# Four-slice tiles for the MoE activations, and a fixed place for the query products, in a linear-attention + MoE kernel

## The chip, the cores and the metric

The kernel runs on one core of a Trainium2 chip. The metric is device time in microseconds (us) of one execution; the median of three runs is compared. A profiled execution is one more run with the hardware profiler on; its trace lists each instruction with its engine, start, duration and what it waited for. The engines are TensorE (PE, with its weight loads listed apart as PEld), VectorE (DVE), ScalarE (ACT), GpSimd (POOL) and SyncE (SP), whose queue issues the DMAs.

## The reference, cut to what matters

There are 8 batches with 8 heads of 576 positions and 64 dimensions; a feature has 128 columns, the model 512, the hidden layer 1024.

```python
def phi(x):
    proj = np.einsum('bhsd,df->bhsf', x, w_phi)
    proj = proj - np.max(np.abs(proj), axis=-1, keepdims=True)
    return np.concatenate([np.exp(proj), np.exp(-proj)], axis=-1)
q_p, k_p = (phi(q), phi(k))
kv = np.einsum('bhsf,bhsd->bhfd', k_p, v)
z = np.sum(k_p, axis=2)
num = np.einsum('bhsf,bhfd->bhsd', q_p, kv)
den = np.einsum('bhsf,bhf->bhs', q_p, z)[..., None] + 1e-06
x = num / den                       # heads side by side: (8, 576, 512)
...
h = np.maximum(x @ w_in, 0.0)
conv_out = sum over k of conv_w[k] * h shifted by k - 1 along the positions
gate = 1.0 / (1.0 + np.exp(-conv_out))
out = h * gate @ w_out
```

## The kernel before

**Attention.** A unit is two head pairs of a batch (16 units, `2 * b + qd`), cut into 5 groups of positions; a group has the running number j. For the keys, `k_process` projects a group (`kp`, lines 223 to 225), takes both exponentials (`ke`) and multiplies them with v into the sums `kv` in PSUM (lines 275 and 279). For the queries, `q_process` projects with two passes over a PSUM tile (lines 360 and 364), finds the largest magnitude of each position on DVE and ACT (lines 368 to 379), and a DMA writes these maxima back into two rows of the operand (line 380, `qx<-qmp`). A third pass on PE then subtracts them in PSUM (line 386). ACT takes the exponentials (line 397) and splits them into a high part and, with DVE, a low part (`qh`, `ql`, lines 60 and 65). The products of the queries with kv (`nm`, lines 418 and 426) follow, and the kv products of the keys five groups later are chained in between them with `after`. ACT copies denominator and numerators out (lines 444 and 449), a DMA spreads the denominator (`den<-dr`, line 447), and `x_process` divides and splits the result into `xh` and `xl`. The first four units project in another way, without a third pass, so third passes exist for the groups 20 to 79.

**MoE.** A part n is half of a batch's positions (288, with one more on either side for the convolution: 290). `h_part` computes eight slices of 128 hidden columns, 12 matmuls each (line 499), and ACT evacuates each from PSUM with a Relu into a tile `h` of its own (line 506); there are `NH` = 11 such tiles, and before slice `8 n + f` is evacuated the planner waits for the gate of slice `8 n + f - 11` (line 504). `conv_process` runs the convolution of each slice on POOL and DVE into `c`, one tile of eight slices (lines 522 and 527), one sigmoid over all eight on ACT (line 531), the product with h slice by slice on DVE (line 535), and the split into `gh` (ACT, line 60) and `gl` (DVE, line 65) slice by slice (line 544). `gh` and `gl` are tiles of four slices with two buffers each, so a part's halves take the places of the part before, once `o_part` has read these. `o_part` computes the output in four blocks of 24 matmuls (line 558), which ACT evacuates (`os`, line 563) and a DMA writes out. `moe_process` runs h_part(n) before o_part(n - 1).

**The order.** Each of these processes is a generator. A planner at the end of the function keeps a model clock `now` and steps one process at a time, by what is ready (`until`, `set_ready`) and by how much attention and MoE work is left; the instructions are recorded in that order, with priorities. The scheduler of the framework then lays out each engine's queue by these priorities and its own timeline model, and sets the semaphores; buffers are given out as it goes. An edge added by hand with `behind(ins, other)` only fixes the order of two instructions on one engine. Before the change there is one such edge per group: the third pass of group j comes behind the first pass of group j + 1 (lines 363 and 388).

Of the kernel before, what the change touches and what calls it, by code (L numbers as in the profile page):

```python
# [7 lines left out]
F32 = mybir.dt.float32  # L8
F32R = mybir.dt.float32r
I32 = mybir.dt.int32  # L10
U32 = mybir.dt.uint32
AF = mybir.ActivationFunctionType
ALU = mybir.AluOpType
# [7 lines left out]
TC = 288  # L21
HW = TC + 2
VW = D + 1
NH = 11

WINDOW = 16
LAT = 1.7
# [8 lines left out]
def kernel(  # L36
# [20 lines left out]
    def split(src, hi, lo, eng_hi, eng_lo):  # L57

        if eng_hi is nc.scalar:
            nc.scalar.activation(out=hi, in_=src, func=AF.Copy)  # L60
        elif eng_hi is nc.gpsimd:
            nc.gpsimd.tensor_scalar(out=hi, in0=src, scalar1=1.0, scalar2=0.0, op0=ALU.mult, op1=ALU.add)  # L62
        else:
            nc.vector.tensor_copy(out=hi, in_=src)
        eng_lo.tensor_tensor(out=lo, in0=src, in1=hi.bitcast(F32), op=ALU.subtract)  # L65
# [108 lines left out]
    def until(*keys):  # L174
        return ("until", [k for k in keys if k is not None])

    def set_ready(key, ns=0):
        ready[key] = now[0] + ns * LAT
# [140 lines left out]

    den = {}  # L320
    numt = {}
    firsts, third = {}, {}

    def behind(ins, other):

        tc.add_manual_dep(ins.ins, other.ins.name,
                          mybir.DependencyInfo(mybir.DependencyClass.NoSync, mybir.DependencyReason.DATA),
                          reason="a group's third pass behind the next group's first")
    xh, xl = {}, {}

    def q_process(b, qd, g):
# [11 lines left out]
        if lo is None:  # L343
            pr = project(n, hi, lo, b, qd, g, "q")
            yield pe(330 * n)
            yield wait(1700)
            yield until(back("num", 2))
            set_ready(("tp", *divmod(j, 5)))

            tp = pg.tile([P, 2, n, P], F32, name=f"tp{b}_{qd}_{g}", tag="gq", bufs=2)  # L350
            for t in range(n):
                for i in range(2):
                    nc.tensor.transpose(out=tp[:, i, t, :], in_=pr[:, 2 * t + i, :], identity=idn)
            yield pe(220 * n)
        else:
            x = hi
            tp = pg.tile([P, 2, n, P], F32, name=f"qp{b}_{qd}_{g}", tag="gq", bufs=2)
            tpf, xf = tp.rearrange("p i t s -> p (i t s)"), x.rearrange("p i s -> p (i s)")
            c = w // 32
            first = nc.tensor.matmul(out=tpf, lhsT=wq_hi, rhs=xf, start=True, stop=False, skip_group_check=True)  # L360
            firsts[j] = first
            if j - 1 in third:
                behind(third.pop(j - 1), first)
            nc.tensor.matmul(out=tpf, lhsT=wq_lo, rhs=xf, start=False, stop=False, skip_group_check=True)

            mt = sb.tile([P, 4, 16], F32, name=f"qmt{b}_{qd}_{g}", tag="qmt", bufs=2)
            with tc.high_priority():
                nc.vector.tensor_reduce(out=mt[:, 0, 0:c], in_=tpf.rearrange("p (c f) -> p c f", f=32), axis=AX,
                                        op=ALU.max, apply_absolute_value=True, apply_transpose=True)
                for a in range(1, 4):  # L370
                    nc.scalar.activation(out=mt[0:32, a, 0:c], in_=mt[32 * a : 32 * a + 32, 0, 0:c], func=AF.Copy)
                m = sb.tile([32, 32], F32, name=f"qm{b}_{qd}_{g}", tag="qm", bufs=2)
                mp = mx[j % 2]
                mr = mt[0:32, :, 0:c].rearrange("p a c -> p c a")
                nc.vector.tensor_reduce(out=mp[:, 0:c].bitcast(F32R), in_=mr, axis=AX, op=ALU.max)
                nc.vector.tensor_reduce(out=m[:, 0:c], in_=mr, axis=AX, op=ALU.max)
                nc.vector.tensor_tensor(out=mp[:, c : 2 * c].bitcast(F32R), in0=m[:, 0:c], in1=mp[:, 0:c], op=ALU.subtract)
                mpt = sb.tile([32, 32], F32, name=f"qmp{b}_{qd}_{g}", tag="qmp", bufs=2)
                nc.vector.transpose(out=mpt, in_=mp)
                nc.sync.dma_start(out=xf[D : D + 2, :].bitcast(F32).rearrange("k (c t) -> k c t", t=32), in_=mpt[0 : 2 * c, :])  # L380
            yield pe(230 * n)
            yield wait(4000)
            yield until(back("num", 2))
            set_ready(("tp", *divmod(j, 5)))
            with tc.high_priority():
                third[j] = nc.tensor.matmul(out=tpf, lhsT=wq_m, rhs=xf, start=False, stop=True, skip_group_check=True)
            if j + 1 in firsts:
                behind(third.pop(j), firsts[j + 1])
            yield pe(115 * n)
        f32 = 2 * b + qd < NKV_F32 or g == 0  # L390
        qh = sb.tile([P, 2, 2, n * P], F32 if f32 else F32R, name=f"qh{b}_{qd}_{g}", tag="qh", bufs=2)
# [18 lines left out]
        for pr_, o, s0, w in parts:  # L410
            for i in range(2):
                khi, klo, kf = kv[b, qd][i]
                k = 0
                for s in range(2):
                    c_ = slice(pr_ * VW, (pr_ + 1) * VW)
                    a, x = (kf if f32 else khi)[:, s, c_], qh[:, s, i, o : o + w]
                    if f32:
                        ins = after(ins, lambda: nc.tensor.matmul(out=ps[:, i, o : o + w], lhsT=a, rhs=x,
                                                                  start=(s == 0), stop=(s == 1)))
                        if paired:  # L420
                            for _ in range(n):
                                ins = after(ins, lambda: next(kvgen[j + 5], ins))
                        continue
                    l, y = klo[:, s, c_], ql[:, s, i, o : o + w]
                    for w_, x_ in ((a, x), (a, y), (l, x)):
                        ins = after(ins, lambda: nc.tensor.matmul(out=ps[:, i, o : o + w], lhsT=w_, rhs=x_,  # L426
                                                                  start=(k == 0), stop=(k == 5)))
                        k += 1
                        if paired and k % 3 > 0:
                            ins = after(ins, lambda: next(kvgen[j + 5], ins))  # L430
                yield pe(6 * max(w / 2.4, 55) + (4 * 160 if paired else 0))
# [56 lines left out]
    def h_part(n):  # L488
        b, c = divmod(n, 2)
        yield until(*[("x", b, p, c) for p in range(4)], "w_in")  # L490
        spawn(conv_process(n))
        for f in range(8):
            ps = pm.tile([P, HW], F32, name=f"hp{n}_{f}", tag="m")
            k = 0
            for p in range(4):
                xa, xb = xh[b, p, c], xl[b, p, c]
                wa, wb = win_hi[p][:, f * P : (f + 1) * P], win_lo[p][:, f * P : (f + 1) * P]
                for w_, x_ in ((wa, xa), (wa, xb), (wb, xa)):
                    nc.tensor.matmul(out=ps, lhsT=w_, rhs=x_, start=(k == 0), stop=(k == 11))  # L499
                    k += 1  # L500
                if p % 2 == 1:
                    yield pe(740)
            if 8 * n + f >= NH:
                yield until(("gate", 8 * n + f - NH))
            hs = sb.tile([P, HW], F32, name=f"h{n}_{f}", tag="h", bufs=NH)
            nc.scalar.activation(out=hs, in_=ps, func=AF.Relu)  # L506
            ht[n, f] = hs
            set_ready(("hs", n, f), 500)
        set_ready(("h", n))

    def conv_process(n):
        c = n % 2
        o = 0 if c == 0 else HW - TC
        for f in range(8):
            yield until(("hs", n, f), ("g4", n - 1) if n > 0 else None)
            if f == 0:
                c4 = sb.tile([P, 8, TC], F32, name=f"c{n}", tag="c", bufs=1)
            hs = ht.pop((n, f))
            ct[n, f] = hs, c4
            cv = c4[:, f, :]  # L520

            nc.gpsimd.tensor_scalar(out=cv, in0=hs[:, o : o + TC], scalar1=cw[:, f, 1:2], scalar2=0.0,  # L522
# [6 lines left out]
                                               op0=ALU.mult, op1=ALU.add)  # L529
        yield wait(2000)  # L530
        nc.scalar.activation(out=c4, in_=c4, func=AF.Sigmoid)  # L531
        for f in range(8):
            set_ready(("gate", 8 * n + f))
            hs, c4 = ct[n, f]
            nc.vector.tensor_tensor(out=c4[:, f, :], in0=c4[:, f, :], in1=hs[:, o : o + TC], op=ALU.mult)
        yield wait(3000)
        yield until(("o", n - 1) if n > 0 else "w_out")
        for f in range(8):
            hs, c4 = ct.pop((n, f))
            if f % 4 == 0:  # L540
                gh4 = sb.tile([P, 4, TC], F32R, name=f"gh{n}_{f}", tag="gh", bufs=2)
                gl4 = sb.tile([P, 4, TC], F32R, name=f"gl{n}_{f}", tag="gl", bufs=2)
            gt[n, f] = gh4[:, f % 4, :], gl4[:, f % 4, :]
            split(c4[:, f, :], *gt[n, f], nc.scalar, nc.vector)
        set_ready(("g4", n))
        set_ready(("g", n), 3000)

# [165 lines left out]
```

## Time and profile before

| | |
|---|---|
| median of 3 runs | 838.35 us (834.71 to 839.17) |
| profiled execution, its own time | 837.11 us |
| its span in the trace | 835.3 us |
| mean granted TensorE clock | 0.984 |
| busy: PE, DVE, ACT, POOL | 781.6, 666.5, 635.3, 310.3 us |

The span runs from the first to the last instruction; the time of the execution also has what lies around it, 1.8 us here. Busy time is the union of an engine's instructions, so overlaps count once, and a PE that is busy throughout can still differ in how closely its matmuls follow each other. A row of instructions names the line, the engine, the operation, the tiles (written <- read), the shape and the count.

### The profile page before, as it was taken

How to read it: one execution, taken by the hardware profiler on the slowest of the kernel's cores; microseconds unless marked ns; L12 is line 12 of the kernel's file. 1: busy time of each engine (PE TensorE's matmuls, PEld its weight loads, DVE VectorE, ACT ScalarE, POOL GpSimd, SP SyncE). 2: the span in 40 equal slices, each digit the busy share in tenths (PEclk: the TensorE clock that was granted, in tenths of full speed). 3: DMA queues.
4: the chain of work that ended last, by engine and by line, in shares of the span. 5: the costliest groups of instructions: out<-in, count | busy, mean ns of one | idle time of the engine just before them, and what ended most of it. 6: DMA issues, size and time to landing. Idle time of an engine off the chain costs nothing.

```text
span 835.3 us, 17596 instructions
## 1 busy us (share of the span) xinstructions
PE 781.6 (94%) x5972; PEld 746.7 (89%) x5972; DVE 666.5 (80%) x1570; ACT 635.3 (76%) x1468; POOL 310.3 (37%) x395
## 2 busy tenths in 40 slices
PE   7888889799999999988999899999999999999998
PEld 7776789799989898988999899899999999999998
DVE  6898998888868878888879688887987978766551
ACT  4787877959878897887888878888797888844332
POOL 5765463252524434233344242433424232211110
PEclk9998989999999999999999999999999999999999
DMA  5643422112221222222222221212221110000001
GB/s 167 183 131 113 126 75 77 48 38 65 62 64 53 63 80 76 67 69 60 77 66 74 71 68 54 73 56 69 62 81 54 56 46 23 11 30 29 22 22 43
DMA packets 66817, 56.46 MB, mean 68 GB/s; under 512 B 17832, under 2 KB 64680, under 8 KB 66728
## 3 DMA queue, kind: packets, MB, share of 16 engines
q1 hardware_dynamic: 66728, 55.35, 22.9%
q8 instruction: 47, 0.77, 0.4%
q14 instruction: 42, 0.34, 0.1%
HBM read 45.21 MB, written 9.44 MB: 65 GB/s over the span
## 4 chain that ended last, share of the span: by engine, by line
PE 32%; ACT 13%; DVE 9%; issue 4%; DMA 4%; POOL 1%; SPq 1%; ACTq 0%; POOLq 0%; DVEq 0%
PE op L558 12%; PE hp L499 11%; PE nm L426 3%; PE kv L279 3%; DVE c L527 2%; ACT qe L397 2%; DMA den<-dr 2%; ACT qh L60 1%; DVE ql L65 1%; ACT gh L60 1%; ACT dr L444 1%; ACT num L449 1%; ACT qx L199 1%; ACT c L531 1%; ACT L397 1%
## 5 line engine op out<-in xcount | busy, mean ns | idle before, releaser
L279 PEld LDWEIGHTS kv<-v,ke 128*128 128x128 f32 x1024 | 157.2, 195 | 10.6 <-ACT ke L260 3.4
L279 PE MATMUL kv<-v,ke 128*128 128x65 f32 x1024 | 163.6, 256 | 2.4 <-ACT ke L260 2.2
L527 DVE SCALAR_TENSOR_TENSOR c<-h,cw,c 128x288 f32<-128x288 f32 (+1 forms) x256 | 143.8, 572 | 26.2 <-POOL c L522 24.6
L499 PE MATMUL hp<-xh,win_hi 128*128 128x290 f32 x512 | 154.5, 303 | 4.6 <-ACT os L563 3.0
L558 PE MATMUL op<-gh,wout_hi 128*128 128x288 f32 x512 | 152.8, 299 | 2.4 <-ACT os L563 2.4
L499 PE MATMUL hp<-xl,win_hi 128*128 128x290 f32 x512 | 152.9, 299 | 0.0
L499 PE MATMUL hp<-xh,win_lo 128*128 128x290 f32 x512 | 152.5, 298 | 0.0
L558 PE MATMUL op<-gh,wout_lo 128*128 128x288 f32 x512 | 152.0, 297 | 0.0
L558 PE MATMUL op<-gl,wout_hi 128*128 128x288 f32 x512 | 151.9, 297 | 0.0
L522 POOL TENSOR_SCALAR c<-h,cw 128x288 f32<-128x288 f32 x128 | 81.5, 640 | 183.5 <-ACT h L506 145.0
L200 POOL TENSOR_TENSOR qx<-qr,qx 64x512 fp32r<-64x512 f32 (+1 forms) x60 | 75.5, 1258 | 162.8 <-ACT qx L199 144.5
L65 DVE TENSOR_TENSOR ql<-qe,qh 128x512 fp32r<-128x512 f32 x112 | 86.5, 788 | 27.0 <-ACT qh L60 26.8
L499 PEld LDWEIGHTS hp<-xh,win_hi 128*128 128x128 f32 x512 | 97.4, 191 | 7.6 <-ACT os L563 4.7
L558 PEld LDWEIGHTS op<-gh,wout_hi 128*128 128x128 f32 x512 | 96.7, 189 | 3.7 <-ACT os L563 3.1
L499 PEld LDWEIGHTS hp<-xl,win_hi 128*128 128x128 f32 x512 | 97.9, 191 | 0.4
L499 PEld LDWEIGHTS hp<-xh,win_lo 128*128 128x128 f32 x512 | 97.7, 191 | 0.4
L558 PEld LDWEIGHTS op<-gh,wout_lo 128*128 128x128 f32 x512 | 96.9, 189 | 0.4
L558 PEld LDWEIGHTS op<-gl,wout_hi 128*128 128x128 f32 x512 | 96.8, 189 | 0.4
L62 POOL TENSOR_SCALAR kxh<-kr 128x256 fp32r<-128x256 f32 (+1 forms) x80 | 40.5, 507 | 119.5 <-PE kp L224 50.5
L65 DVE TENSOR_TENSOR gl<-c,gh 128x288 fp32r<-128x288 f32 x128 | 55.5, 485 | 22.6 <-ACT gh L60 22.5
L506 ACT ACTIVATE h<-hp 128x290 f32<-128x290 f32 x128 | 50.4, 404 | 30.3 <-PE hp L499 29.8
L426 PE MATMUL nm<-ql,kvh 128*65 128x256 f32 x224 | 69.2, 309 | 2.2 <-DVE ql L65 2.2
(99 smaller groups left out, 1936.4 us busy)
## 6 DMA issues: line engine op xcount, KB each, us to landing
qr<-in_qT_dram SPq DMA_DIRECT2D x112, 128.0 KB
v<-in_vt_dram SPq DMA_DIRECT2D x80, 130.0 KB
out_dram<-os SPq DMA_DIRECT2D x64, 144.0 KB
kr<-in_kT_dram SPq DMA_DIRECT2D x64, 128.0 KB
w_r<-in_w_in_dram SPq DMA_DIRECT2D x8, 512.0 KB
w_r<-in_w_out_dram SPq DMA_DIRECT2D x8, 512.0 KB
rr<-rc SPq DMA_DIRECT2D x128, 2.2 KB
qr<-in_qT_dram SPq DMA_DIRECT2D x28, 64.0 KB
```

The costliest lines, as they stand in the source:

```text
L60: nc.scalar.activation(out=hi, in_=src, func=AF.Copy)
L62: nc.gpsimd.tensor_scalar(out=hi, in0=src, scalar1=1.0, scalar2=0.0, op0=ALU.mult, op1=ALU.add)
L65: eng_lo.tensor_tensor(out=lo, in0=src, in1=hi.bitcast(F32), op=ALU.subtract)
L200: nc.gpsimd.tensor_tensor(out=x[D:P], in0=raw[D:P], in1=x[D:P].bitcast(F32), op=ALU.subtract)
L279: ins = nc.tensor.matmul(out=kp[i][:, s, p0 : p0 + VW], lhsT=lhsT, rhs=v[:, (2 * t + i) * VW : (2 * t + i + 1) * VW], start=False, stop=(g ...
L397: nc.scalar.activation(out=e, in_=tps, func=AF.Exp, scale=1.0 - 2.0 * s)
L426: ins = after(ins, lambda: nc.tensor.matmul(out=ps[:, i, o : o + w], lhsT=w_, rhs=x_, start=(k == 0), stop=(k == 5)))
L499: nc.tensor.matmul(out=ps, lhsT=w_, rhs=x_, start=(k == 0), stop=(k == 11))
L506: nc.scalar.activation(out=hs, in_=ps, func=AF.Relu)
L522: nc.gpsimd.tensor_scalar(out=cv, in0=hs[:, o : o + TC], scalar1=cw[:, f, 1:2], scalar2=0.0, op0=ALU.mult, op1=ALU.add)
L527: nc.vector.scalar_tensor_tensor(out=cv[:, lo:hi], in0=hs[:, o + j - 1 + lo : o + j - 1 + hi], scalar=cw[:, f, j : j + 1], in1=cv[:, lo:hi ...
L558: nc.tensor.matmul(out=ps, lhsT=w_, rhs=x_, start=(k == 0), stop=(k == 23))
```

## The change

Two things change.

The tile `h` now holds four slices, with `NH` = 3 tiles. ACT still evacuates each slice by itself, and the convolution still reads single slices. The product with the sigmoid becomes two DVE instructions over four slices each instead of eight over one, and the split becomes two copies on ACT and two subtractions on DVE over four slices each. The planner waits for a tile's place three tiles back, by halves of a part.

On PE, the first product of the queries of group j with kv (`nms[j]`) is ordered behind the third pass of group j + 1, whichever of the two is recorded later. The rest of that block is chained behind its first product by `after`, as before. `third` is no longer emptied, since it is needed twice.

```diff
-NH = 11
+NH = 3
...
-                behind(third.pop(j - 1), first)
+                behind(third[j - 1], first)
...
             if j + 1 in firsts:
-                behind(third.pop(j), firsts[j + 1])
+                behind(third[j], firsts[j + 1])
+            if j - 1 in nms:
+                behind(nms[j - 1], third[j])
...
                         ins = after(ins, lambda: nc.tensor.matmul(out=ps[:, i, o : o + w], lhsT=w_, rhs=x_,
                                                                   start=(k == 0), stop=(k == 5)))
+                        if j not in nms:
+                            nms[j] = ins
+                            if j + 1 in third:
+                                behind(ins, third[j + 1])
...
-            if 8 * n + f >= NH:
-                yield until(("gate", 8 * n + f - NH))
-            hs = sb.tile([P, HW], F32, name=f"h{n}_{f}", tag="h", bufs=NH)
-            nc.scalar.activation(out=hs, in_=ps, func=AF.Relu)
-            ht[n, f] = hs
+            if f % 4 == 0:
+                if 2 * n + f // 4 >= NH:
+                    yield until(("gate", 2 * n + f // 4 - NH))
+                h4 = sb.tile([P, 4, HW], F32, name=f"h{n}_{f}", tag="h", bufs=NH)
+            nc.scalar.activation(out=h4[:, f % 4, :], in_=ps, func=AF.Relu)
+            ht[n, f] = h4
...
-        for f in range(8):
-            set_ready(("gate", 8 * n + f))
-            hs, c4 = ct[n, f]
-            nc.vector.tensor_tensor(out=c4[:, f, :], in0=c4[:, f, :], in1=hs[:, o : o + TC], op=ALU.mult)
+        for k in range(2):
+            set_ready(("gate", 2 * n + k))
+            h4, c4 = ct[n, 4 * k]
+            cq = c4[:, 4 * k : 4 * k + 4, :]
+            nc.vector.tensor_tensor(out=cq, in0=cq, in1=h4[:, :, o : o + TC], op=ALU.mult)
         yield wait(3000)
         yield until(("o", n - 1) if n > 0 else "w_out")
-        for f in range(8):
-            hs, c4 = ct.pop((n, f))
-            if f % 4 == 0:
-                gh4 = sb.tile([P, 4, TC], F32R, name=f"gh{n}_{f}", tag="gh", bufs=2)
-                gl4 = sb.tile([P, 4, TC], F32R, name=f"gl{n}_{f}", tag="gl", bufs=2)
-            gt[n, f] = gh4[:, f % 4, :], gl4[:, f % 4, :]
-            split(c4[:, f, :], *gt[n, f], nc.scalar, nc.vector)
+        for k in range(2):
+            h4, c4 = ct[n, 4 * k]
+            gh4 = sb.tile([P, 4, TC], F32R, name=f"gh{n}_{k}", tag="gh", bufs=2)
+            gl4 = sb.tile([P, 4, TC], F32R, name=f"gl{n}_{k}", tag="gl", bufs=2)
+            split(c4[:, 4 * k : 4 * k + 4, :], gh4, gl4, nc.scalar, nc.vector)
+            for f in range(4 * k, 4 * k + 4):
+                gt[n, f] = gh4[:, f % 4, :], gl4[:, f % 4, :]
+                ct.pop((n, f))
```

More of the change, by code (lines that the diff above doesn't have):

```diff
@@ L321 @@
     numt = {}
-    firsts, third = {}, {}
+    firsts, third, nms = {}, {}, {}
     def behind(ins, other):
@@ L327, in behind @@
                           mybir.DependencyInfo(mybir.DependencyClass.NoSync, mybir.DependencyReason.DATA),
-                          reason="a group's third pass behind the next group's first")
+                          reason="behind a later group's pass")
     xh, xl = {}, {}
@@ L427, in q_process @@
                                                                   start=(k == 0), stop=(k == 5)))
+                        if j not in nms:
+                            nms[j] = ins
+                            if j + 1 in third:
+                                behind(ins, third[j + 1])
                         k += 1
@@ L517, in conv_process @@
                 c4 = sb.tile([P, 8, TC], F32, name=f"c{n}", tag="c", bufs=1)
-            hs = ht.pop((n, f))
-            ct[n, f] = hs, c4
+            h4 = ht.pop((n, f))
+            ct[n, f] = h4, c4
+            hs = h4[:, f % 4, :]
             cv = c4[:, f, :]
```

## The prediction

> **What bounds the kernel now.** I read the head of the page first, then the busy time in five stretches, then what TensorE (PE) waited for, then single rows of the timeline.
>
> ```profile
> span 835.3 us, 17596 instructions
> PE 781.6 (94%) x5972; PEld 746.7 (89%) x5972; DVE 666.5 (80%) x1570; ACT 635.3 (76%) x1468; POOL 310.3 (37%) x395
> 0.00:140.00 140.00, 120.45 (x814) 106.86 (x815) 123.76 (x231) 103.11 (x220) 83.14 (x102) 0.94 0.43 125
> 140.00:300.00 160.00, 148.25 (x1148) 142.48 (x1146) 133.01 (x323) 130.71 (x303) 62.45 (x75) 0.97 0.21 60
> 300.00:500.00 200.00, 189.55 (x1520) 182.25 (x1519) 163.44 (x405) 168.51 (x408) 76.61 (x99) 1.00 0.25 70
> 500.00:720.00 220.00, 212.34 (x1672) 205.04 (x1672) 182.66 (x459) 185.44 (x438) 72.50 (x92) 1.00 0.19 56
> 720.00:835.00 115.00, 110.98 (x827) 110.03 (x825) 63.64 (x153) 47.56 (x103) 15.62 (x29) 1.00 0.08 27
> ```
>
> In the stretches the columns after the length are PE, weight load, DVE, ACT, POOL, then clock, DMA share and GB/s. PE is the bound, at 94%; nothing in the change removes a matmul. So only PE's idle time can be won. It is 19.6 us before 140 us, where the gate and the split have not started (rows below: 158.7 and later), and after that 11.8 + 10.5 + 7.7 + 4.0 = 34 us. That is the ceiling for the whole change: about 803 us. DVE runs at 83% and ACT at 84% between 140 and 720 us, so the rest of PE's idling should be work that arrives late there. PE's own waits from 140 us on say which:
>
> ```profile
> PE qp L386 <- DMA qx<-qmp: 5.7, 7, 1.6
> PE qp L360 <- POOL qx L200: 4.7, 5, 1.6
> PE kp L223 <- ACT num L449: 4.0, 3, 2.9
> PE hp L499 <- ACT os L563: 3.0, 7, 0.8
> PE op L558 <- ACT os L563: 2.4, 2, 1.6
> PE nm L426 <- DVE ql L65: 2.0, 3, 0.9
> PE nm L426 <- ACT qh L60: 1.8, 3, 1.1
> PE kv L279 <- ACT ke L260: 1.5, 3, 1.0
> PE nm L426 <- ACT num L449: 1.4, 4, 0.6
> PE kp L223 <- DVE ks L230: 1.3, 2, 1.1
> ```
>
> (total us, times, longest). These ten rows are 27.8 us. ACT and DVE ended 17.4 of them, a DMA and POOL 10.4. No row names the gate (L535), and none of these ten the split of the gated tile: they reach PE only by standing in front of something else.
>
> **Part 1, fewer and longer instructions.** The 128 gate products and 128 subtractions on DVE become 32 each, the 128 copies on ACT become 32. Durations overlap at the seams, so I take start to start.
>
> ```profile
> L535 DVE TENSOR_TENSOR c<-c,h x128: 416/450/1556, 158.7 to 813.1; 128x288 f32<-128x288 f32 x128
> L65 DVE TENSOR_TENSOR gl<-c,gh x128: 390/447/1535, 163.8 to 820.5; 128x288 fp32r<-128x288 f32 x128
> L60 ACT ACTIVATE gh<-c x128: 425/429/448, 161.8 to 819.9; 128x288 fp32r<-128x288 f32 x128
> 759.72 3.04 DVE L535 TENSOR_TENSOR c<-c,h 128x288 f32<-128x288 f32 x8 [1.55 <-ACT c L531]
> 650.30 0.68 DVE L65 TENSOR_TENSOR ql<-qe,qh 128x512 fp32r<-128x512 f32 x1
> 655.12 1.28 DVE L65 TENSOR_TENSOR ql<-qe,qh 128x512 fp32r<-128x512 f32 x2
> 731.13 2.13 ACT L531 ACTIVATE c<-c 128x2304 f32<-128x2304 f32 x1
> ```
>
> DVE: eight gates take 3.04 us, so the pitch is (3.04 - 0.45) / 7 = 0.37 us for 288 elements. Two of 512 take 1.28, so the pitch there is 1.28 - 0.68 = 0.60 us. The slope is 0.23 / 224 = 1.03 ns an element, the fixed part 0.37 - 0.30 = 0.07 us. One instruction of 1152 elements then has a pitch of 1.26 us and lasts 1.34. Four old ones have 1.48; three fixed parts, 0.21 us, go, 64 times: 13.4 us of DVE, 1.6% of the span. The maxima of 1.5 us show single slices slowed by something else at the time; grouping doesn't remove that.
>
> ACT: from 0.43 us at 288 to 2.13 at 2304 elements the slope is 0.84 ns, so 1152 elements last 1.16 us. The pitch of the small ones is in the next rows.
>
> ```profile
> 738.70 1.45 ACT L60 ACTIVATE gh<-c 128x288 fp32r<-128x288 f32 x4 [1.14 <-PE op L558]
> 740.30 1.45 ACT L60 ACTIVATE gh<-c 128x288 fp32r<-128x288 f32 x4 [0.15 <-PE op L558]
> 741.65 0.39 ACT L563 ACTIVATE os<-op 128x288 f32<-128x288 f32 x1
> 741.57 0.30 PE L499 MATMUL hp<-xh,win_lo 128*128 128x290 f32 x1
> 742.10 0.40 PE L499 MATMUL hp<-xh,win_hi 128*128 128x290 f32 x1 [0.23 <-ACT os L563]
> ```
>
> (1.45 - 0.43) / 3 = 0.34 us; four have 1.36, the long one about 1.07 (1.16 less the same 0.09 of overlap). That is 0.29 us less, 32 times 9.3 us of ACT. These rows also show the one place where the relief meets PE directly. The copies of a part wait until the output products of the part before have read the old halves; the last evacuation (os) stands behind them, and the next part's matmul waits for its PSUM buffer. At PE's pitch of 0.13 us the matmul at 742.10 was due at 741.70. With the second copy ending its turn at 740.30 + 1.07 = 741.37, os starts 0.28 us sooner and the stall of 0.4 falls to 0.1. The two rows "<- ACT os" count nine such waits: **-2.5 us**, between 0 (another instruction takes the room) and 5.4 (all of it). As the four copies already run as one block, the long copy holds ACT's queue no longer than they did.
>
> Whether the later first slice hurts depends on when PE comes for it. Before, slice 0 was complete one copy and one subtraction after the start, 0.43 + 0.45 = 0.9 us; now it takes 1.16 + 1.34 = 2.5 us.
>
> ```profile
> 765.36 3.17 DVE L65 TENSOR_TENSOR gl<-c,gh 128x288 fp32r<-128x288 f32 x8 [2.60 <-ACT gh L60]
> 779.71 0.30 PE L558 MATMUL op<-gh,wout_hi 128*128 128x288 f32 x1
> 817.28 1.45 ACT L60 ACTIVATE gh<-c 128x288 fp32r<-128x288 f32 x4 [1.14 <-PE op L558]
> 817.75 3.17 DVE L65 TENSOR_TENSOR gl<-c,gh 128x288 fp32r<-128x288 f32 x8 [4.20 <-ACT gh L60]
> 818.81 0.29 PE L558 MATMUL op<-gl,wout_hi 128*128 128x288 f32 x1
> ```
>
> Part 13 splits until 768.5 and PE comes at 779.7: 11 us of cover, since the h products of part 14 run before the output products of part 13. The last part has none, since o(14) is followed by o(15) at once. Its first low product starts at 818.81; the grouped low half would be there at 817.28 + 2.5 = 819.8. **+1.0 us**, once, and no other work is left to fill it. Without the cover it would be 1.0 us in each of 16 parts.
>
> The Trainium skill, in "Perfetto Trace Analysis", section Optimizing Scalar/DVE Operations, speaks against this part: where the vector and scalar engines aren't saturated but make bubbles elsewhere, it advises to break instructions up, so that work is done sooner. At 80% and 76% busy the page's case is ours; the trace follows it at the last part alone, and by the rule everywhere the sum would end near 847 instead (rival D).
>
> What is left of the relief lies in the attention stretch, between other work of the two queues. Of the ACT and DVE waits 17.4 - 5.4 = 12 us are not os; they fall on 18 times, 0.7 us each. A gate or a split that stands in such a chain is now 0.4 us shorter (two instructions' saving of 0.21). If one stands in a third of the chains, 18 x 0.4 / 3: **-2.4 us**, between 0 (in none) and -7.2 (in each).
>
> The rings of h: 3 tiles of 4 slices are 12 slices for 11. The evacuation of slice 4 of a part now waits for the first gate of the part before, where slice 3 waited for its slice 0: one slice later (12 matmuls, 1.6 us) against a gate that ends 0.9 us later. I put it at nothing; POOL's convolution reads single slices still.
>
> **Part 2, order on PE.** No instruction is added; the first query product of group j-1 (nm) must follow the third pass (L386) of group j. First and last of the groups where it stands ahead of it now, 39 of the 60:
>
> ```profile
> 178.75 0.28 PE L418 MATMUL nm<-qh,kvf 128*65 128x64 f32 x2
> 186.57 0.50 PE L386 MATMUL qp<-qx,wq_m 128*128 128x512 f32 x1 [1.57 <-DMA qx<-qmp]
> 704.77 0.28 PE L426 MATMUL nm<-qh,kvh 128*65 128x256 f32 x1
> 715.29 0.40 PE L386 MATMUL qp<-qx,wq_m 128*128 128x512 f32 x1
> ```
>
> These move, with the kv products chained into them, their copies of the denominator and numerator on ACT, and the issue of den<-dr on SP, which comes behind the qx<-qmp of the group after. What nm waits for itself (qh, ql, num: 5.2 us) shrinks as it starts later: 39/60 of it is 3.4. Against it stands the third pass, which waits for its DMA (7 times, 0.8 us): an nm block ahead of it was cover, and everything in PE's queue stands still behind it. If each of the 39 lost that cover, 39 x 0.8 = 32 us. MoE matmuls can take its place; the buffer nm shares with the k projection also frees later (the row kp <- num). I take 3.4 - 1.4: **-2 us**, between -3.4 and +32.
>
> **Sum:** 837.1 (the profiled execution's own time, 835.3 of it span) - 2.5 + 1.0 - 2.4 - 2 = 831.2. The median shown, 838.35, is 1.2 above that execution, so 832 on its scale.
>
> **The rivals.**
> B, the relief is off the path. The two queues keep gaps of their own in front of the work that PE waits for, or DMA and POOL make it as late. Then only os and the tail count: 838.35 - 2.5 + 1.0 = 837. For it: no row names gate or split. Against: 12 us of waits on the two queues that become shorter.
> C, slower: the third pass loses its cover. Place: L386 in the moved groups. Price: 0.8 us. For it: the row at 186.57 waited 1.6 us for its DMA even with an nm block ahead. Against: only 7 waits in 60. If half of the 39 wait: +16 us on 832, 848; it takes the sum past no change from 8 such waits (6.4 us) on and past +0.5% from 13.
> D, the late first slice costs 1.0 us at all 16 parts, not at one: 832 + 15 = 847. The 11 us of cover speak against it.
> E, the four slices of h4 are ordered as one tile:
>
> ```profile
> L522 POOL TENSOR_SCALAR c<-h,cw 128x288 f32<-128x288 f32 x128 | 81.5, 640 | 183.5 <-ACT h L506 145.0
> 743.06 1.07 DVE L527 SCALAR_TENSOR_TENSOR c<-h,cw,c 128x288 f32<-128x288 f32 x2 [0.71 <-POOL c L522]
> ```
>
> Then the Relu of a slice waits for the convolution of the slice before, 0.64 + 1.07 us, which with the 0.4 us of the Relu itself makes 2.1 us a slice against PE's 1.6. Beside attention that is hidden; in the three parts after 720 us it is 3 x 6 x 0.5 = 9 us: 841. Against: c is one tile of eight slices today, and POOL waits there for h, not for DVE's work on the slice before.
> F, the reverse: most of the queueing goes, 12 + 3.4 + 2.5 - 1.0 = 17 us: 821.
>
> **How the numbers follow.** A measurement of this kernel can tell about 0.5% from no change, 4.2 us: below 834.2 is faster, above 842.5 slower. Forecast 0.45, F 0.06: faster 0.51. B 0.27, E 0.02: no change 0.29. C 0.17, D 0.03: slower 0.20. The forecast's own range is 826 to 837; the range given, 819 to 847, takes in F and C's lesser half.
>
> **What would show it.** Right: 32 gates and 32 subtractions near 1.3 us, 32 copies near 1.16; "hp <- ACT os" and "op <- ACT os" down from 5.4 to about 3; a stall near 1 us at the last part's first low product; every nm behind the next third pass, with nm's waits down by half. Wrong: "qp L386 <- DMA qx<-qmp" above 12 us (C), PE waiting for gl at other parts (D), ACT h waiting for POOL (E), or PE's idle time after 140 us unchanged though DVE and ACT are 10 us less busy (B).

## The result, and the profile after

The changed kernel took 828.6 us in the median (825.1 to 830.0 in the runs compared) against 837.6 us for the kernel before beside it: a ratio of 0.9897, 95% interval 0.9859 to 0.9935. That is 1.0% less time, 9 us; 832 us was forecast, within 819 to 847. A median here and below counts slow runs too where there were any (one of 1460 us here; the other three have a median of 827.25), while ranges and ratios leave them out. Its profiled execution took 827.25 us, 9.9 us less than the one before.

First the head of the page, and busy time up to 140 us and from there to the end (PE, weight load, DVE, ACT, POOL, then clock, DMA share, GB/s). The changed kernel:

```profile
span 825.5 us, 17295 instructions
PE 775.8 (94%) x5972; PEld 744.0 (90%) x5972; DVE 649.4 (79%) x1378; ACT 627.4 (76%) x1372; POOL 316.1 (38%) x395
0.00:140.00 140.00, 118.85 (x810) 104.55 (x811) 123.32 (x231) 102.50 (x220) 82.96 (x102) 0.94 0.43 125
140.00:825.50 685.50, 657.00 (x5165) 639.40 (x5163) 526.11 (x1148) 524.90 (x1153) 233.13 (x294) 0.99 0.20 57
```

The same stretch of the kernel before:

```profile
140.00:835.30 695.30, 661.13 (x5161) 639.80 (x5158) 542.76 (x1339) 532.23 (x1249) 227.19 (x294) 0.99 0.19 56
```

After 140 us PE is idle for 685.5 - 657.0 = 28.5 us, where it was 695.3 - 661.1 = 34.2. So 5.7 us of the 9.8 are idle time, and 4.1 us are matmuls that follow each other more closely, since their number is nearly the same (5165 and 5161). DVE is 17.1 us and ACT 7.9 us less busy. Now PE's waits from 140 us on in the changed kernel (total, times, longest), which answer to the ten rows of before:

```profile
PE op L572 <- ACT os L577: 5.0, 3, 4.2
PE qp L360 <- POOL qx L200: 3.8, 4, 1.1
PE qp L386 <- DMA qx<-qmp: 3.4, 4, 1.4
PE hp L509 <- ACT h L517: 3.3, 6, 1.5
PE kp L223 <- ACT num L459: 3.1, 2, 2.6
PE kv L279 <- ACT ke L260: 2.1, 2, 1.6
PE qp L360 <- ACT qe L399: 1.1, 1, 1.1
PE op L572 <- DVE gl L65: 0.9, 1, 0.9
PE op L572 <- ACT h L517: 0.9, 1, 0.9
PE nm L432 <- ACT num L459: 0.4, 2, 0.2
PE hp L509 <- ACT os L577: 0.3, 1, 0.3
```

The three large rows of nm (5.2 us before) are down to 0.4; the seven waits of hp for os (3.0) to one of 0.3. New are one single wait of 4.2 us of an output product for os, more waits of hp for its Relu (3.3 us, 0.9 before), and the wait for gl at the last part. Line numbers of the MoE part are 10 to 14 higher than before.

The grouped instructions, by shape (busy, mean ns of one, idle before and its cause):

```profile
L65 DVE TENSOR_TENSOR gl<-c,gh 128x1152 fp32r<-128x1152 f32 x32 | 44.2, 1383 | 28.4 <-ACT gh L60 28.2
L548 DVE TENSOR_TENSOR c<-c,h 128x1152 f32<-128x1152 f32 x32 | 43.7, 1405 | 14.8 <-ACT c L543 14.8
L60 ACT ACTIVATE gh<-c 128x1152 fp32r<-128x1152 f32 x32 | 37.0, 1163 | 9.0 <-PE op L572 8.6
```

And the order on PE, in the timeline of the changed kernel, at two pairs of groups, an early one and a late one:

```profile
184.49 0.40 PE L386 MATMUL qp<-qx,wq_m 128*128 128x512 f32 x1
184.73 0.28 PE L420 MATMUL nm<-qh,kvf 128*65 128x64 f32 x2
...
699.59 0.40 PE L386 MATMUL qp<-qx,wq_m 128*128 128x512 f32 x1
700.89 0.28 PE L432 MATMUL nm<-qh,kvh 128*65 128x256 f32 x1
```

nm stands behind the third pass of the next group at all 60 places, often at once (within 0.3 us at 27 of them; in the first pair above, 0.24 us later). Before, it stood ahead at 39.

### The profile page after: what moved, and what is told of

The parts are those of the page before. It is cut to its first block, busy times and chain, and to the rows that moved or that the text cites. A ratio compares the mean times of both kernels' runs of the same rounds, so it can differ in the third digit from the quotient of the medians.

```text
span 825.5 us, 17295 instructions
## 1 busy us (share of the span) xinstructions
PE 775.8 (94%) x5972; PEld 744.0 (90%) x5972; DVE 649.4 (79%) x1378; ACT 627.4 (76%) x1372; POOL 316.1 (38%) x395
## 5 line engine op out<-in xcount | busy, mean ns | idle before, releaser
L279 PE MATMUL kv<-v,ke 128*128 128x65 f32 x1024 | 161.4, 256 | 4.3 <-ACT ke L260 4.2
L200 POOL TENSOR_TENSOR qx<-qr,qx 64x512 fp32r<-64x512 f32 (+1 forms) x60 | 77.6, 1294 | 111.2 <-ACT qx L199 102.3
L65 DVE TENSOR_TENSOR ql<-qe,qh 128x512 fp32r<-128x512 f32 x112 | 90.0, 822 | 22.0 <-ACT qh L60 21.7
L62 POOL TENSOR_SCALAR kxh<-kr 128x256 fp32r<-128x256 f32 (+1 forms) x80 | 42.3, 529 | 130.8 <-issue 62.6
L517 ACT ACTIVATE h<-hp 128x290 f32<-128x290 f32 x128 | 50.8, 405 | 40.1 <-PE hp L509 39.6
L432 PE MATMUL nm<-qh,kvl 128*65 128x256 f32 x224 | 69.2, 309 | 0.0
```

The lines of the kernel that those rows point to most:

```text
L200: nc.gpsimd.tensor_tensor(out=x[D:P], in0=raw[D:P], in1=x[D:P].bitcast(F32), op=ALU.subtract)
L279: ins = nc.tensor.matmul(out=kp[i][:, s, p0 : p0 + VW], lhsT=lhsT, rhs=v[:, (2 * t + i) * VW : (2 * t + i + 1) * VW], start=False, stop=(g ...
L517: nc.scalar.activation(out=h4[:, f % 4, :], in_=ps, func=AF.Relu)
```

## The experiments

Ratios are against the kernel before, measured beside each set on the same chip, with 95% intervals. The theory under test is the prediction's: the grouping wins about 4 us, the order 2. Two rivals go with it: that the order does it all, and one that the prediction had not thought of, that any edit that makes the scheduler lay out the queues anew moves the time by as much.

**The grouping alone.** The changed kernel without its two uses of the new edge:

```diff
-            if j - 1 in nms:
-                behind(nms[j - 1], third[j])
...
-                            if j + 1 in third:
-                                behind(ins, third[j + 1])
```

> Part 1 alone: tiles of four slices with the grouped gate and split, no edge between the query products and the next third pass. The prediction's sum gives -2.5 + 1.0 - 2.4 = -3.9 us against the kernel before, about 833.7. Rival 'the order does it all': within 1 us of the kernel before. Rival 'the new layout of the queues, not the parts': anything within 5 us on either side, with PE waits in other places than os. In each case the last part's first low product should wait about 1.1 us for gl, as in the changed kernel.

Measured: 843.3 us, ratio 1.0088 (1.0053 to 1.0122). It is slower, by 7 us where 4 us less were expected. PE's waits in this kernel from 140 us on:

```profile
PE op L566 <- ACT os L571: 10.0, 5, 3.1
PE qp L386 <- DMA qx<-qmp: 6.0, 6, 2.9
PE kp L223 <- ACT num L453: 5.4, 7, 2.6
PE nm L428 <- ACT qh L60: 3.4, 3, 1.6
```

The waits of hp for os are gone here too (no such row is among the large ones), but output products now wait 10 us for os, at five places with up to 3.1 us. The local effect came as forecast, and more than its worth was lost elsewhere. At all five places the os stands on ACT behind the sigmoid of a part (2.13 us), at four of them with other copies and exponentials in between. The two waits of op for os in the kernel before, 2.4 us, stand behind a sigmoid as well. So 7.6 us more waits fell at this one kind of place, which the change does not touch. DVE is 14 us and ACT 6 us less busy than before, and PE's idle time after 140 us is 700.7 - 662.7 = 38.0 us against 34.2.

**The order alone.** The new edge in the kernel before, with its single slices (the same lines as in the diff of the change, without `NH`, `h_part` and `conv_process`).

> Part 2 alone: the edge added to the kernel before, single-slice tiles kept. The prediction's sum gives -2 us, about 835.6. Rival 'the order does it all': -9 us, about 828.6, with the third passes a steady 8 to 10 us apart and the query products right behind each. If the two parts only help together, this is no faster than before and the sum of this and the run of part 1 alone falls short of -9. The tail's wait for gl should not be there.

Measured: 830.2 us, ratio 0.9918 (0.9886 to 0.9950), 6.9 us faster: nearly "the order does it all". Busy time from 500 to 720 us in this kernel:

```profile
500.00:720.00 220.00, 217.83 (x1748) 213.05 (x1747) 190.87 (x477) 193.33 (x456) 79.55 (x97) 1.00 0.21 58
```

PE idles there for 2.2 us, where it was 7.7 before, and runs 76 matmuls more in the same time. From 140 us to the end its idle time is 29.5 us against 34.2, with the same busy time (661.0 and 661.1). The waits of its third passes from 140 us on rose only a little:

```profile
PE qp L386 <- DMA qx<-qmp: 7.8, 8, 2.3
PE nm L432 <- ACT num L459: 2.0, 3, 1.5
PE hp L509 <- ACT os L573: 0.7, 3, 0.2
```

7.8 us against 5.7 before: cover was lost, by 2 us, not by the 16 of rival C. The waits for os, 5.4 us in nine before, are 0.7 us in three here, without any grouping.

**The last part's split by slice.**

```diff
-            split(c4[:, 4 * k : 4 * k + 4, :], gh4, gl4, nc.scalar, nc.vector)
+            if n < 2 * B - 1:
+                split(c4[:, 4 * k : 4 * k + 4, :], gh4, gl4, nc.scalar, nc.vector)
+            else:
+                for f in range(4):
+                    split(c4[:, 4 * k + f, :], gh4[:, f, :], gl4[:, f, :], nc.scalar, nc.vector)
```

> The changed kernel with the split of the last part alone taken slice by slice again. The prediction's own term: 1.0 us less than the changed kernel, the wait of the last part's first low product (1.08 us there) gone, nothing else moved, about 827.6. If the wait only moves to the slices of the second half, less than 0.3 us is won.

Measured: 825.5 us, ratio 0.9851 (0.9820 to 0.9882); the span of its profile is 824.0 us against 825.5. The place itself, in the timeline of the changed kernel, ACT, DVE and PE:

```profile
806.27 1.17 ACT L60 ACTIVATE gh<-c 128x1152 fp32r<-128x1152 f32 x1 [1.14 <-PE op L572]
807.47 1.36 DVE L65 TENSOR_TENSOR gl<-c,gh 128x1152 fp32r<-128x1152 f32 x1 [5.40 <-ACT gh L60]
807.67 0.29 PE L572 MATMUL op<-gh,wout_hi 128*128 128x288 f32 x1
808.89 0.40 PE L572 MATMUL op<-gl,wout_hi 128*128 128x288 f32 x1 [0.92 <-DVE gl L65]
```

and with the last split by slice:

```profile
807.36 0.30 PE L576 MATMUL op<-gh,wout_hi 128*128 128x288 f32 x1
807.50 0.29 PE L576 MATMUL op<-gl,wout_hi 128*128 128x288 f32 x1
```

The first low product started 1.22 us after the high one, and now 0.14: 1.08 us won, 1.0 was forecast. The wait does not come back at the second half. The medians are 3.1 us apart, but the intervals of the two ratios overlap, so no more than the 1.08 us is put down to this edit. The rest of the layout stayed much as it was: the last nm product starts at 711.9 us, in the changed kernel at 712.2, and the wait of 4.2 us for os is in both.

**Rings of 12 and of 10 in the kernel before.** No work changes, `NH` alone.

```diff
-NH = 11
+NH = 12
```

> The kernel before with 12 single-slice tiles for h instead of 11: no instruction is added, removed or made longer, only the ring has the size of the changed kernel's. The prediction put the ring at nothing: within 1 us of before, about 838, if the plan of the queues stays much the same. Rival 'layout': if a plan that is laid out anew scatters by itself, this moves by 3 us or more in either direction, and so much of the 1% can't be told from chance.

> The kernel before with 10 single-slice tiles for h. No work is changed. If the size of the ring has an effect of its own (12 was 7 us slower), 10 should be faster, by some us. If the plan without the edge merely scatters when it is laid out anew, it lands anywhere from -7 to +9 us with waits in other places, with no order in 10, 11, 12.

Measured: with 12, 844.5 us, ratio 1.0088 (1.0055 to 1.0120); with 10, 834.5 us, ratio 0.9979 (0.9960 to 0.9999). So 10, 11 and 12 give -0.2%, 0 and +0.9%, for the same instructions. They come in the order of the size, so these three alone do not rule out an effect of the ring itself. One row of PE's waits with the ring of 12, which was 4.0 us in 3 times with 11:

```profile
PE kp L223 <- ACT num L449: 8.0, 4, 2.9
```

The ring sets when the planner steps the MoE part, and the queues are laid out anew behind that: nm stands ahead of the next third pass at 29, 39 and 30 of the 60 places with 10, 11 and 12 tiles. Such single waits fall in other places then.

**The ring of 12 with the edge.** The order alone, `NH = 12`.

> The edge of part 2 and 12 single-slice tiles for h, no grouping: the kernel with the edge alone, with the changed kernel's ring. Theory 'the ring itself costs': slower than the edge alone by about 7 us as it was without the edge, 837. Theory 'the ring of 12 was one unlucky layout, and the edge makes the layout steadier': within 3 us of the edge alone, 828 to 833. What is left between this and the changed kernel (828.6) is then the grouping.

Measured: 830.0 us, ratio 0.9925 (0.9900 to 0.9950), the same as the order alone (0.9918). With the edge no effect of the ring is seen. That the 7 us without it belonged to one layout and not to the size of the ring fits this.

**The edge turned round.** In the changed kernel:

```diff
-                behind(nms[j - 1], third[j])
+                behind(third[j], nms[j - 1])
...
-                                behind(ins, third[j + 1])
+                                behind(third[j + 1], ins)
```

> The changed kernel with the edge turned round: the third pass of group j must follow the first query product of group j-1. If it is the early third pass and the later query products that win (prediction: nm's own waits shrink), this loses it: nm waits for qh, ql and num of 5 us or more, 836 to 845. If any fixed order of the two would do, it stays at 826 to 831. It is the one most likely to show more waits of the third pass in PE's queue behind nm, not for its DMA.

Measured: 833.3 us, ratio 0.9965 (0.9938 to 0.9991). It lies between the kernel before and the changed one, less slow than expected. PE's waits from 140 us on:

```profile
PE nm L432 <- ACT qh L60: 4.3, 6, 1.8
PE qp L386 <- DMA qx<-qmp: 1.6, 3, 0.8
PE nm L432 <- DVE ks L230: 1.3, 1, 1.3
PE nm L432 <- ACT num L459: 0.9, 2, 0.6
```

nm's own waits are back (6.5 us in these three rows against 0.4), the third pass waits for its DMA less (1.6 against 3.4). In the time, the direction is the smaller part: against the same grouping with no edge (1.0088), the edge turned round is 1.2% less and the edge of the change 1.9%. So the rival that any fixed order of the two would do holds for much of it, as far as one layout of each can tell.

**The split by slice in all parts.** The changed kernel, with the gate grouped and the edge kept:

```diff
-            split(c4[:, 4 * k : 4 * k + 4, :], gh4, gl4, nc.scalar, nc.vector)
+            for f in range(4):
+                split(c4[:, 4 * k + f, :], gh4[:, f, :], gl4[:, f, :], nc.scalar, nc.vector)
```

> The changed kernel with the split slice by slice in all parts; four-slice tiles, grouped gate and edge stay. By the prediction's sizes the split has half of DVE's saving (6.7 us) and all of ACT's (9.3): os waits at the start of a part (about 0.4 us each, seven times) come back, the tail's 1.08 goes, so +2.5 - 1.0 + 1.2 = about 2.7 us slower than the changed kernel, 831. If the grouping is worth nothing, it is 1 us faster (the tail alone), 827.5.

Measured: 843.3 us, ratio 1.0100 (1.0067 to 1.0133). Neither size expected can explain that. The largest difference in the trace is one wait that came 13 times, 17.4 us in all against 3.3 in the changed kernel; the spans differ by 19.4 us. From 382 to 678 us it comes about every 49 us, with 1.6 to 1.7 us each. PE's row, and one of the places on ACT and PE:

```profile
PE hp L509 <- ACT h L517: 17.4, 13, 1.7
379.27 0.27 ACT L454 ACTIVATE dr<-nm 1x128 f32<-1x128 f32 x1
379.56 0.44 ACT L459 ACTIVATE num<-nm 64x64 f32<-64x64 f32 x2
380.01 0.27 ACT L454 ACTIVATE dr<-nm 1x128 f32<-1x128 f32 x1
380.31 0.22 ACT L459 ACTIVATE num<-nm 64x64 f32<-64x64 f32 x1
380.43 0.62 ACT L60 ACTIVATE qh<-qe 128x512 fp32r<-128x512 f32 x1
381.06 0.21 ACT L459 ACTIVATE num<-nm 64x64 f32<-64x64 f32 x1
381.30 0.72 ACT L517 ACTIVATE h<-hp 128x290 f32<-128x290 f32 x2
381.77 0.40 PE L509 MATMUL hp<-xh,win_hi 128*128 128x290 f32 x1 [1.68 <-ACT h L517]
```

Two hidden slices wait in PSUM while ACT runs the copies behind a group of 64 positions, and PE, with both buffers full, stands still. The layout has settled into a pattern that keeps meeting this place; the last nm product starts 42.6 us later than in the changed kernel (754.8 against 712.2 us). Why the scheduler's plan falls into it here and not with the grouped split is not settled.

**The grouped split alone, with the edge.** The order alone, its split changed as in the change (`h` in single slices, gate by slice).

> The edge of part 2, eleven single-slice tiles and a gate slice by slice; only the split is grouped. By the prediction's sizes against the edge alone (830.2): os waits at the start of a part go (-2.5 at most, fewer here), half of DVE's relief, the tail's wait for gl comes (+1.1): 828 to 830. If the slow run with the split ungrouped (843.3) was one unlucky layout, this stays within 3 us of the edge alone; if the grouped split is what keeps the layout good, this is the faster side, 826 or less.

Measured: 831.4 us, ratio 0.9950 (0.9927 to 0.9973): within 3 us of the edge alone, on the slow side, if at all. In this kernel the grouped split is not worth the 15 us that lie between the split ungrouped (843.3) and the changed kernel (828.6), so most of those belong to a layout of its own.

**The output's evacuation first, and the Relu's too.** On the kernel with the last split by slice:

```diff
-            nc.scalar.activation(out=os_, in_=ps, func=AF.Copy)
+            with tc.high_priority():
+                nc.scalar.activation(out=os_, in_=ps, func=AF.Copy)
```

> The changed kernel with the last part's split by slice (825.5) and, new, the evacuation of the output products (os) at high priority, so that it isn't queued on ACT behind sigmoid and table loads. Theory: the one wait of 4.2 us of an output product for os goes, and the rest of 'op <- ACT os': -4 to -5 us, about 821. Rival 'layout': the waits move to other pairs and the time stays within 3 us of 825.5.

and, besides, the same three lines around the Relu into h:

> As the run with os first, and the Relu evacuation of the hidden slices (h) at high priority too: it waits on ACT behind the six copies that follow the group of 64 columns. Theory: 'hp <- ACT h' (3.3 us) and 'op <- ACT h' (0.9) go as well: about 817 to 820. Rival: attention's copies and exponentials come later by as much, PE waits for num, qh and ke instead, and it is no faster than 825 or slower.

Measured: 822.4 us, ratio 0.9849 (0.9820 to 0.9877), and 820.6 us, ratio 0.9822 (0.9798 to 0.9846). PE's waits for the two evacuations, with os first:

```profile
PE hp L509 <- ACT h L517: 3.5, 4, 1.7
PE op L576 <- ACT os L582: 1.8, 2, 1.6
PE hp L509 <- ACT os L582: 1.4, 1, 1.4
```

and with both first:

```profile
PE hp L509 <- ACT h L518: 3.5, 4, 1.7
PE nm L432 <- ACT num L459: 3.2, 3, 2.5
```

The wait of 4.2 us is gone, but half of its worth came back as others, and the waits for the Relu stayed at 3.5 us with the priority on: that theory fell. Against the last split by slice alone (0.9851) neither differs beyond the intervals; with os first, the ratio is the same (0.9849), as its rival had it. The second is the fastest median of all; it beats the kernel before by 1.8% and the changed kernel by 0.75%, with intervals that do not meet.

**Another layout of the same work.** On the kernel with the last split by slice, `AHEAD = 290` for 300.

> The changed kernel with the last part's split by slice (825.5) and the attention's priority lead set to 290 instead of 300: no work changes, the queues are laid out anew in places. Theory 'the edge makes the layout steady': within 2 us of 825.5. Rival: it scatters by 5 us or more, as the kernel before did with rings of 10, 11 and 12.

Measured: 822.2 us, ratio 0.9839 (0.9814 to 0.9863). That is 3.3 us less than 825.5, more than the 2 us of its theory and less than the 5 of its rival; by the ratios, which allow for the kernel before on each chip, the two are 1 us apart (0.9851 and 0.9839). The wait of 4.2 us for os is not there either (two waits, 0.9 us), with no priority given: it belonged to one layout. So nothing of the 822.4 us with os first can be put down to the priority.

## Why the prediction was right, and where it was not

The time and its direction were right; the shares of the two parts were not. That the sum came out near is in part luck: measured alone, the parts were +7 and -7 us where -3.9 and -2 were forecast, which adds up to nothing, and together they made -9.

**The grouped instructions.** 1.34 us was forecast for DVE and 1.38 and 1.40 came, 1.16 for ACT and 1.163 came. The relief of DVE was 17 us (13.4 forecast), of ACT 8 (9.3).

**-2.5 us from os at the start of a part.** The place was read rightly for seven of the nine waits: each of the seven of hp has four copies of gh on ACT ahead of the os. The two of op (1.6 us at 464 us, 0.8 at 706) have none; they stand behind a sigmoid, so the term should have been seven times 0.28, 2.0 us. The seven became one in the changed kernel, 0.3 us for 3.0. But with the order alone, without a long copy, only three of 0.2 us are left, at 737, 763 and 790 us. So with the edge in place the long copies are seen to win 0.7 us, and the rest of the gain at this place comes with the edge too. The sum of both os rows is 5.3 us, as 5.4 before, since one wait of 4.2 us, until 643.42 us, came behind another sigmoid. There ACT ran a table load, the sigmoid and another table load (1.28, 2.13 and 1.28 us, from 635.09 us on), then exponentials and copies of attention, and the os at 642.96.

**+1.0 us at the last part.** Shown by the trace and by its removal: 1.08 us. At other parts no wait for gl appears, so rival D did not come. There the first half of gl was complete 12 us or more before PE's first product with it. The Trainium skill's advice to break instructions up where Scalar and Vector are not saturated but cause bubbles on other engines ("Perfetto Trace Analysis", section Optimizing Scalar/DVE Operations) holds at this one part, with its 1.08 us; no wait for gl shows a price of grouping at the others.

**-2.4 us from shorter queues.** Not shown. Without the edge, the grouping ran 0.9% slower, as did the ring of 12 that shortens nothing. With the edge, two layouts of the grouping with the last split by slice stand at 0.9851 and 0.9839 against 0.9918 and 0.9925 for two without it: 0.7 to 0.9% less, about 6 us, near the forecast -3.9 - 1.0 of the whole grouping without its tail. But the changed kernel itself (0.9897) differs from the order alone by 0.2%, with intervals that overlap, and the split alone grouped (0.9950) and the gate alone grouped (1.0100) gain nothing. So much can be said: with the edge, the grouping of both has the lower medians in the layouts tried; that the shorter queues are the cause was only argued.

**-2 us from the order.** This is the term that was mis-sized: alone it is worth 6.9 us. The step counted nm's own waits and took off a price for lost cover. The waits did go (5.2 to 0.4 us in the changed kernel, 2.0 for num with the edge alone), and the price was about 2 us with the edge alone and nothing in the changed kernel (3.4 us of DMA waits against 5.7). What it did not count is other waits that go with the edge: those for os, 5.4 us before and 0.7 with the edge alone, which the sum had given to the grouping, and between 500 and 720 us, where PE idles 5.5 us less, also small ones of k and q projections. Turned round, the edge is 4.7 us slower than in the changed kernel, with nm's waits back, but still 10 us faster than the same grouping without it: its direction is the smaller part of its worth. That the third pass, taken first, lets the exponentials start sooner fits this, but no run tried that by itself.

**The rivals.** B, 837 us, and C, 848, did not come; C's price per wait was right and only a few waits came. For the grouping alone B's sign did come: PE's idle time did not fall though DVE and ACT were less busy. E did not come: with the sliced tile the Relu waits on ACT for PE alone (39.6 us in 42 waits). F's size was reached by later versions, not by the change. What was missing among them is the scatter of the layout: three rings in the kernel before, with the same work, differ by 1.1%, as much as the whole gain. Without the edge four layouts (rings of 10, 11, 12, and the grouping) lie at 0.998 to 1.009; with it as in the change, three without the whole grouping at 0.992 to 0.995, and the five with it (the last split by slice or not, two with evacuations first) at 0.982 to 0.990. These eight do not overlap with the four, which speaks for more than scatter, though some of the five share most of their layout; the ninth, with the gate alone grouped, at 1.010, shows that the edge is no guarantee.

**Open.** Why the grouping alone is slower (its own cost or one bad layout that puts os behind the sigmoid more often), how much of the edge's worth any fixed order would bring, and what puts the layout with the gate alone grouped into its cycle.

## What to carry to other kernels

Where a scheduler lays out the queues from a model, a change of nothing but a buffer count can move the time by 1%, so a small gain is judged over several layouts of the same work, not over one. An edge that fixes the order of two steps of a pipeline (the short pass that starts a long chain ahead of the bulk product that ends one) was worth more here than 14 us less work on an engine that does not bind. Grouped instructions made no consumer wait where it came 12 us or more after the first of them was done; at the last one, which has nothing to hide behind, they are worth taking apart.

## What the runs showed of the hardware that was not expected

In one run, the ring of 12 with the edge, the granted clock is recorded at 0.936 over the span and 0.95 in the last stretch, and the matmuls are no slower for it. Its last stretch and one of its groups of matmuls:

```profile
720.00:828.20 108.20, 103.90 (x773) 102.95 (x771) 56.97 (x136) 43.30 (x93) 12.39 (x24) 0.95 0.09 29
L509 PE MATMUL hp<-xh,win_hi 128*128 128x290 f32 x512 | 153.6, 301 | 5.1 <-ACT h L516 3.7 <-ACT os L573 0.7 <-ACT xh L60 0.5
```

and the last stretch of the changed kernel, with a clock of 1.00:

```profile
720.00:825.50 105.50, 100.88 (x748) 99.87 (x746) 52.12 (x84) 38.64 (x63) 13.29 (x24) 1.00 0.09 29
```

773 matmuls in 108.2 us are 0.140 us each, 748 in 105.5 are 0.141. The mean of the group is 301 ns, and 302 in the changed kernel. What the lower recorded clock stands for is not shown.
